# Second mixture's output products kind by kind over the row tiles of a chunk, in an attention and two-mixture kernel on one core

## The chip, the core and the metric

The kernel runs on one core of a Trainium2 chip. The metric is the device time of one execution in microseconds (us). The core has five engines: TensorE (PE, matrix products; its weight loads are listed as PEld), VectorE (DVE), ScalarE (ACT), GpSimd (POOL) and SyncE (SP, which here issues DMAs).

## The reference

Three stages follow each other. Attention over q, k, v of shape (4, 8, 576, 64) with a threshold: scores below the row maximum minus tau are dropped. The result, 2304 tokens of width 512, goes into a first mixture (512 to 1024 and back to 512 with a normalisation), and that into a second one, which is what the change touches:

```python
def _moe2_ref(x, w_in, w_out):
    h = x @ w_in                                        # 2304 x 512 by 512 x 2048
    g = np.maximum(h, 0.0) + np.log1p(np.exp(-np.abs(h)))
    return (g @ w_out).astype(np.float32)               # 2304 x 2048 by 2048 x 512
```

## The kernel before, in words

Matrix products use a high and a low part of every fp32 operand: x is split into `xh` and `xl`, the weights into `w2h`, `w2l` and `wo2h`, `wo2l`, g into `gh` and `gl`. A product of two numbers is made of three kinds, high by high, high by low and low by high, which are summed up in PSUM.

The second mixture goes over five blocks of tokens, four of 512 and one of 256, and in each over 16 chunks of 128 of the 2048 hidden columns. One chunk of one block has three steps.

- `m2_h` (line 573): twelve products into one PSUM bank give h for 128 hidden columns and all tokens of the block. ScalarE then takes Abs (L582) and Exp (L583), VectorE an add (L584) and a subtraction (L585), and ScalarE Ln (L586).
- `m2_g1`: VectorE takes a maximum and a sum (L591) and a subtraction (L592), ScalarE rounds to `gh` (L593), and VectorE forms `gl` (L594).
- `m2_y` (line 612): for each row tile j of 128 tokens, four in a large block and two in the last, three products of 128 x 512 into the bank `y{j}`. The bank collects all 16 chunks of a block. After the last chunk it is copied to `yo` (L616), by VectorE for even j and by ScalarE for odd j, and stored by a DMA that SP issues (L619).

The loop at the end of the function runs over all (block, chunk) pairs and looks two ahead: step i has `m2_h` of pair i, `m2_g1` of pair i - 1 and `m2_y` of pair i - 2. During block 0, `next(pw, 0)` also converts one chunk of w2_out per step (lines 80 to 88, on ScalarE, VectorE and POOL). In the later steps of a block, the x of the next one is loaded and split (L536, L541, L542).

The tile framework lays out the order of each engine when the program is built, and an engine's order in the trace deviates from the source in places. For instance, ScalarE runs Abs of the next chunk ahead of `gh` of this one.

Buffers that matter: four banks for h, one bank for each of `y0` to `y3`, three buffers each for `gh` and `gl`, and two for `yo`. So the first product into `y{j}` of a new block waits for the copy of the old `y{j}`, and the copy of tile 2 waits until the store of tile 0 has read its `yo`.

Of the kernel before, what the change touches and what calls it, by code (L numbers as in the profile page):

```python
# [21 lines left out]
P = 128  # L22
# [11 lines left out]
def tile_attention_solu_softplus(ctx: ExitStack, tc: tile.TileContext, q, k, v, tau, w_in, w_out, g_ln, w2_in, w2_out, out):  # L34
    nc = tc.nc
    PSUM = bass.MemoryType.PSUM
    pe, dve, act, pool, sp = nc.tensor, nc.vector, nc.scalar, nc.gpsimd, nc.sync
# [426 lines left out]
    NC2 = FF2 // P  # L464
# [95 lines left out]
    wo2h = [w2b.tile([P, DM], F32R, tag=f"wo2h{c}", name=f"wo2h{c}") for c in range(NC2)]  # L560
    wo2l = [w2b.tile([P, DM], F32R, tag=f"wo2l{c}", name=f"wo2l{c}") for c in range(NC2)]
    pw = prep_w2(w2a, lambda c: w2_out[c * P:(c + 1) * P, :].bitcast(U32), wo2h, wo2l, 2)
    gs = {}
    psy = {}
# [31 lines left out]
    def rows(bi, j):  # L596

        u, t = units[blocks[bi][0] + j // 2], j % 2
        if u == "T":
            return [(S * (2 * t + a) + 512, 64) for a in range(2)]  # L600
        return [(S * u[0] + 256 * u[1] + P * t, P)]

    def m2_y(bi, c):
        gl, gh = gs.pop((bi, c))[3:]
        n = blocks[bi][1]
        if c == 0:
            psy[bi] = [psY.tile([P, 512], F32, tag=f"y{j}", name=f"y{bi}_{j}") for j in range(n // P)]
        for j in range(n // P):
            y = psy[bi][j]
            i = 0  # L610
            for g_, w_ in ((gh, wo2h[c]), (gh, wo2l[c]), (gl, wo2h[c])):
                pe.matmul(y, g_[:, P * j:P * j + P], w_, start=(c == 0 and i == 0), stop=(c == NC2 - 1 and i == 2))  # L612
                i += 1
            if c == NC2 - 1:
                yo = m2.tile([P, DM], F32, tag="yo", name=f"yo{bi}_{j}", bufs=2)
                (act.copy if j % 2 else dve.tensor_copy)(out=yo, in_=y)  # L616
                r0 = 0
                for t0, m in rows(bi, j):
                    sp.dma_start(out=out[t0:t0 + m, :], in_=yo[r0:r0 + m, :])  # L619
                    r0 += m  # L620
# [3 lines left out]
    for i in range(len(seq) + LA):  # L624
        if i < len(seq):
            bi, c = seq[i]
            if bi == 0:
                next(pw, 0)
            if bi + 1 < len(blocks):
                j = (c - 2) // 4  # L630
                if c in (2, 6) and j < blocks[bi + 1][1] // 256:
                    m2_load(bi + 1, j)
                elif c in (4, 8) and j < blocks[bi + 1][1] // 256:
                    m2_split(bi + 1, j)
            m2_h(bi, c)
        if 0 <= i - 1 < len(seq):
            m2_g1(*seq[i - 1])
        if i >= LA:
            m2_y(*seq[i - LA])
# [51 lines left out]
```

## Time and profile before

| | |
|---|---|
| time, median of 3 runs | 1007.86 us (1007.46 to 1009.16) |
| the profiled execution's own time | 1010.33 us |
| its span, first to last instruction | 1008.5 us |
| mean granted TensorE clock in it | 0.971 |
| second mixture in it | about 600 to 1005 us; blocks change near 697, 790, 878 and 958 us |

The rows below come from the profiled execution. Times are counted from the start of its span. "Idle before" in brackets is how long the engine stood idle before an instruction, and behind the arrow is what ended that. A matmul's length contains its pipeline, so the rate of matmuls is read from their starts. A granted clock of 1.00 stands for 2.4 GHz, and 0.50 for 1.2 GHz.

### The profile page before, as it was taken

To read this page: it belongs to the slowest core of one execution; us is meant where nothing else is said; L and a number is where in the kernel's file an instruction comes from. 1 tells how busy PE (TensorE), PEld (TensorE's weight loads), DVE (VectorE), ACT (ScalarE), POOL (GpSimd) and SP (SyncE) were. 2 spreads that over 40 slices of the span, in tenths; PEclk is the share of its full clock that TensorE was granted. 3 is DMA by queue.
4 is the path that set the end of the run, shared out by engine and by line. 5 is a ranking of instruction groups with operands and counts; after the bars stand their busy time and mean duration, and the time that the engine had idled before them with its cause. 6 is when DMAs were issued, how large, how long until landed. Compare 5 with 4: busy or idle time off the path is not lost.

```text
span 1008.5 us, 14610 instructions
## 1 busy us (share of the span) xinstructions
PE 948.4 (94%) x5664; PEld 747.2 (74%) x5664; DVE 713.4 (71%) x1387; ACT 568.9 (56%) x1082; POOL 75.1 (7%) x47
## 2 busy tenths in 40 slices
PE   3898999999999999999997699898999999999997
PEld 2666567777677777876886588676888788888896
DVE  5898866766768577676589959976555755665565
ACT  4765666666657567566556546544444444444453
POOL 0000000000000000000033534311001000000000
PEclk8898899999999999999998799998999999999999
DMA  8412200112001220000054533302000100100010
GB/s 220 173 61 79 75 27 12 35 44 78 27 11 36 65 69 15 12 11 6 33 162 141 162 127 103 125 1 84 1 0 22 63 1 1 42 1 0 1 44 21
DMA packets 27125, 55.21 MB, mean 55 GB/s; under 512 B 3248, under 2 KB 12464, under 8 KB 27056
## 3 DMA queue, kind: packets, MB, share of 16 engines
q1 hardware_dynamic: 26896, 53.99, 17.1%
q8 instruction: 44, 0.72, 0.3%
q10 hardware_dynamic: 160, 0.30, 0.1%
q14 instruction: 25, 0.20, 0.1%
HBM read 44.83 MB, written 9.44 MB: 54 GB/s over the span
## 4 chain that ended last, share of the span: by engine, by line
PE 67%; DVE 18%; ACT 8%; issue 3%; DMA 2%; SPq 0%; DVEq 0%; ACTq 0%
PE y L612 12%; PE h L573 12%; PE s L177 10%; PE w L355 9%; PE w L403 8%; PE w L276 7%; PE w L210 5%; DVE u L82 2%; DVE w L584 2%; DVE t L585 2%; DVE w L591 2%; DMA raw<-in_w_in_dram 2%; DVE u L84 2%; DVE w L592 1%; DVE gl L594 1%
## 5 line engine op out<-in xcount | busy, mean ns | idle before, releaser
L177 PE MATMUL s<-k,q 64*128 64x288 f32 (+1 forms) x640 | 135.0, 445 | 16.8 <-ACT q L143 8.9
L187 DVE TENSOR_REDUCE nm<-s 128x1 f32<-128x576 f32 x144 | 104.5, 750 | 43.4 <-PE s L177 43.4
L573 PE MATMUL h<-x2h,w2h 128*128 128x512 f32 (+1 forms) x320 | 119.3, 375 | 8.6 <-ACT x2h L541 7.0
L188 ACT ACTIVATE E<-s,nm 128x576 f32<-128x576 f32 x128 | 92.5, 741 | 52.6 <-DVE nm L187 52.4
L612 PE MATMUL y<-wo2h,gh 128*128 128x512 f32 x288 | 114.6, 398 | 7.5 <-ACT gh L593 4.3
L573 PE MATMUL h<-x2l,w2h 128*128 128x512 f32 (+1 forms) x320 | 118.8, 371 | 0.8 <-POOL x2l L542 0.8
L573 PE MATMUL h<-x2h,w2l 128*128 128x512 f32 (+1 forms) x320 | 118.6, 371 | 0.0
L612 PE MATMUL y<-wo2h,gl 128*128 128x512 f32 x288 | 113.8, 397 | 4.6 <-DVE gl L594 4.6
L612 PE MATMUL y<-wo2l,gh 128*128 128x512 f32 x288 | 113.4, 394 | 0.0
L195 DVE SCALAR_TENSOR_TENSOR E<-E,etau 128x576 f32<-128x576 f32 x128 | 102.5, 813 | 13.0 <-ACT E L188 9.1
L177 PEld LDWEIGHTS s<-k,q 64*128 64x128 f32 (+1 forms) x640 | 71.1, 182 | 53.8 <-issue 13.1
L586 ACT ACTIVATE w<-w 128x512 f32<-128x512 f32 (+1 forms) x80 | 47.1, 589 | 96.5 <-DVE t L585 96.4
L593 ACT CAST gh<-w 128x512 fp32r<-128x512 f32 (+1 forms) x80 | 46.2, 577 | 84.6 <-DVE w L592 84.3
L212 ACT COPY eT<-w 128x512 f32<-128x512 f32 x128 | 72.0, 592 | 24.2 <-PE w L210 23.7
L403 PE MATMUL w<-lh,wo1h 128*128 128x256 f32 x288 | 83.6, 291 | 0.0
L276 PE MATMUL w<-eT,v 128*64 128x256 f32 (+2 forms) x784 | 83.1, 357 | 0.0
L591 DVE SCALAR_TENSOR_TENSOR w<-h,w 128x512 f32<-128x512 f32 (+1 forms) x80 | 50.9, 637 | 44.7 <-ACT w L586 44.7
L403 PE MATMUL w<-ll,wo1h 128*128 128x256 f32 x288 | 81.5, 283 | 0.0
L403 PE MATMUL w<-lh,wo1l 128*128 128x256 f32 x288 | 81.4, 283 | 0.0
L594 DVE TENSOR_TENSOR gl<-w,gh 128x512 fp32r<-128x512 f32 (+1 forms) x80 | 51.0, 638 | 42.2 <-ACT gh L593 41.5
L276 PEld LDWEIGHTS w<-eT,v 128*64 128x64 f32 x784 | 52.8, 140 | 32.9 <-issue 9.7
L573 PEld LDWEIGHTS h<-x2h,w2h 128*128 128x128 f32 x320 | 61.4, 192 | 20.3 <-ACT x2h L541 7.2
(100 smaller groups left out, 1870.1 us busy)
## 6 DMA issues: line engine op xcount, KB each, us to landing
raw<-in_w_in_dram SPq DMA_DIRECT2D x16, 512.0 KB, 3.5
raw<-in_w_out_dram SPq DMA_DIRECT2D x16, 512.0 KB, 3.5
v<-in_v_dram SPq DMA_DIRECT2D x16, 320.0 KB, 3.0
x2s<-x SPq DMA_DIRECT2D x36, 128.0 KB, 1.7
x2r<-x2s SPq DMA_DIRECT2D x9, 512.0 KB, 4.0
q<-in_q_dram SPq DMA_DIRECT2D x30, 144.0 KB, 3.0
raw<-in_w_in_dram SPq DMA_DIRECT2D x4, 1024.0 KB, 8.9
raw<-in_w_out_dram SPq DMA_DIRECT2D x4, 1024.0 KB, 5.0
```

Source lines behind the costliest of these rows:

```text
L177: pe.matmul(o, z["q"][r, c:c + m], z["k"][r, kc:kc + 288], start=True, stop=True)
L187: dve.tensor_reduce(out=nm, in_=sv, axis=AX.XY, op=ALU.max, negate=True)
L188: act.activation(out=E.rearrange("p (a b) -> p a b", a=2), in_=sv, func=AF.Exp, bias=nm, scale=1.0)
L195: dve.scalar_tensor_tensor(out=E, in0=E, scalar=etau, in1=E, op0=ALU.is_ge, op1=ALU.mult, accum_out=acc)
L212: act.copy(out=eT, in_=bk)
L276: pe.matmul(o[64 * h:64 * h + 64, :], w_, e, start=(i == 0), stop=(i == 4))
L355: pe.matmul(ps, x_[:, c, P * t:P * t + P], w_[:, c, 512 * n:512 * n + 512], start=(j == 0), stop=(j == 11))
L403: pe.matmul(o, w_[:, c, P * m:P * m + P], l_[:, c, :], start=(j == 0), stop=(j == 23))
L573: pe.matmul(ps, w_[:, kc, :], x_[:, kc, 0:n], start=(j == 0), stop=(j == 11))
L591: dve.scalar_tensor_tensor(out=w_, in0=ps, scalar=0.0, in1=w_, op0=ALU.max, op1=ALU.add)
L594: dve.tensor_tensor(out=gl, in0=w_, in1=f(gh), op=ALU.subtract)
L612: pe.matmul(y, g_[:, P * j:P * j + P], w_, start=(c == 0 and i == 0), stop=(c == NC2 - 1 and i == 2))
```

## The change

The three kinds of product of a chunk become the outer loop and the row tiles the inner one. The start flag stands at the first kind of chunk 0 and the stop flag at the last kind of chunk 15, as before. The copies and stores after the last chunk come behind all twelve products in the source.

```diff
         if c == 0:
             psy[bi] = [psY.tile([P, 512], F32, tag=f"y{j}", name=f"y{bi}_{j}") for j in range(n // P)]
+        for i, (g_, w_) in enumerate(((gh, wo2h[c]), (gh, wo2l[c]), (gl, wo2h[c]))):
+            for j in range(n // P):
+                pe.matmul(psy[bi][j], g_[:, P * j:P * j + P], w_, start=(c == 0 and i == 0), stop=(c == NC2 - 1 and i == 2))
         for j in range(n // P):
             y = psy[bi][j]
-            i = 0
-            for g_, w_ in ((gh, wo2h[c]), (gh, wo2l[c]), (gl, wo2h[c])):
-                pe.matmul(y, g_[:, P * j:P * j + P], w_, start=(c == 0 and i == 0), stop=(c == NC2 - 1 and i == 2))
-                i += 1
             if c == NC2 - 1:
```

## Rows read from the trace of the kernel before

**Rows 1.** The page, part 1: busy time, share of span, instructions.
```profile
PE 948.4 (94%) x5664; PEld 747.2 (74%) x5664; DVE 713.4 (71%) x1387; ACT 568.9 (56%) x1082; POOL 75.1 (7%) x47
```

**Rows 2.** The page, part 5: output products, first kind; busy, mean ns | idle before.
```profile
L612 PE MATMUL y<-wo2h,gh 128*128 128x512 f32 x288 | 114.6, 398 | 7.5 <-ACT gh L593 4.3
```

**Rows 3.** Waits, 600 to 1009 us: us in total, times, longest.
```profile
PE y L612 <- DVE gl L594: 4.6, 5, 1.9
PE y L612 <- ACT gh L593: 4.3, 6, 1.7
PE y L612 <- DVE yo L616: 3.2, 3, 1.7
```

**Rows 4.** Timeline of TensorE in block 0: start, length, instruction [idle before].
```profile
634.68 0.51 PE L612 MATMUL y<-wo2h,gl 128*128 128x512 f32 x1 [1.87 <-DVE gl L594]
...
637.01 0.63 PE L612 MATMUL y<-wo2l,gh 128*128 128x512 f32 x1
```

**Rows 5.** Stretches: length, busy PE, PEld, DVE, ACT, POOL, clock, DMA share, GB/s.
```profile
636.30:639.50 3.20, 3.20 (x9) 2.50 (x8) 3.10 (x7) 3.03 (x6) 0.11 (x1) 0.50 0.09 36
...
697.70:704.40 6.70, 5.63 (x13) 3.96 (x14) 4.55 (x9) 3.55 (x7) 0.00 (x0) 0.50 0.42 150
704.50:769.00 64.50, 64.50 (x286) 53.37 (x285) 38.02 (x60) 29.16 (x47) 0.00 (x0) 1.00 0.00 1
789.00:796.00 7.00, 5.31 (x24) 4.02 (x23) 4.85 (x9) 3.50 (x6) 0.00 (x0) 1.00 0.33 121
```

**Rows 6.** Waits, 603 to 697 us, the longest of ScalarE and of VectorE.
```profile
ACT w L586 <- DVE t L585: 20.3, 12, 3.0
...
DVE w L591 <- ACT w L586: 4.2, 6, 0.7
```

**Rows 7.** Timeline of TensorE where blocks change (0/1, 1/2, 2/3).
```profile
696.84 0.47 PE L612 MATMUL y<-wo2h,gh 128*128 128x512 f32 x1 [1.71 <-ACT gh L593]
...
700.58 0.80 PE L612 MATMUL y<-wo2h,gh 128*128 128x512 f32 x1 [1.07 <-DVE yo L616]
...
791.43 0.51 PE L612 MATMUL y<-wo2h,gh 128*128 128x512 f32 x1 [1.69 <-DVE yo L616]
...
879.24 0.50 PE L612 MATMUL y<-wo2h,gh 128*128 128x512 f32 x1 [0.43 <-DVE yo L616]
```

**Rows 8.** Timeline of VectorE at the change from block 0 to 1.
```profile
696.01 0.68 DVE L616 COPY yo<-y 128x512 f32<-128x512 f32 x1
...
697.85 0.69 DVE L585 SCALAR_TENSOR_TENSOR t<-w,t 128x512 f32<-128x512 f32 x1
...
699.84 0.68 DVE L616 COPY yo<-y 128x512 f32<-128x512 f32 x1
```

**Rows 9.** Timeline of ScalarE there, its second copy.
```profile
699.90 0.58 ACT L616 COPY yo<-y 128x512 f32<-128x512 f32 x1 [0.70 <-DMA out_dram<-yo]
```

**Rows 10.** The tile yo: its stores, from issue to landing.
```profile
DMA to landing us min/median/max: 2.0/2.2/4.4
```

**Rows 11.** Chain of waits in block 1: start, length, line; a y and an h chunk.
```profile
712.20 2.72 PE y L612 x12
714.92 2.72 PE h L573 x12
```

**Rows 12.** Timeline of ScalarE in block 4, its last wait for TensorE.
```profile
975.54 0.38 ACT L582 ACTIVATE t<-h 128x256 f32<-128x256 f32 x1 [0.24 <-PE h L573]
```

**Rows 13.** Timeline of the end, engine by engine.
```profile
1003.06 0.50 PE L612 MATMUL y<-wo2h,gh 128*128 128x512 f32 x1 [1.27 <-ACT gh L593]
...
1004.33 0.40 PE L612 MATMUL y<-wo2h,gl 128*128 128x512 f32 x1
1004.07 0.69 DVE L616 COPY yo<-y 128x512 f32<-128x512 f32 x1 [0.60 <-PE y L612]
1004.76 0.58 ACT L616 COPY yo<-y 128x512 f32<-128x512 f32 x1 [1.75 <-PE y L612]
1004.79 0.92 SPq L619 DMA_DIRECT2D out_dram<-yo  x2
```

## The prediction

> **What bounds the kernel now.** I read the page first: TensorE is busy for 94% of the span [rows 1], so a change must either take matmul time away or take away waits of TensorE. The change removes no product: the 864 products of line 612 (three groups of 288) stay, each with its weight load, and the lengths of one are about the same in the three groups, one of which stands in [rows 2]. So I looked at the waits of the second mixture, 600 to 1009 us. TensorE's own waits before line 612 have three releasers: `gl` (4.6 us in 5 waits), `gh` (4.3 us in 6) and the copies `yo` that free the banks of the block before (3.2 us in 3) [rows 3]. These 12.1 us are what an order of the output products can touch. The reader is to see where each of them lies.
>
> The `gl` waits lie in block 0, while w2_out is still being converted on VectorE. The longest is 1.87 us, between the second and the third product of a chunk, and a stretch at half clock follows it [rows 4]: granted clock 0.50 (1.2 GHz) from 636.3 to 639.5 us [rows 5]. The `yo` waits lie where one block of tokens follows another. There TensorE has done the six products of row tiles 0 and 1 of the new block and stands before tile 2, because VectorE has not yet copied the old tile 2 out: 1.07 us at 700.58, 1.69 at 791.43, 0.43 at 879.24 [rows 7]. The `gh` waits lie mainly ahead of 696.84 (1.71 us) [rows 7] and at the end.
>
> Next the question that decides the credit: who waits for TensorE? From 603 to 697 us the list of waits has eight rows of ScalarE and VectorE, and they name each other, POOL and one DMA, never TensorE (the two longest stand in [rows 6]). The chain Abs, Exp, add, subtract, Ln, max, subtract, `gh` runs there at its own pace, and `gh` of chunk 0 of block 1 comes at 696.84 whatever TensorE did before.
>
> **The change, part by part.**
>
> *Later need of `gl`.* A product takes 2.72/12 = 0.227 us [rows 11]. Before, `gl` is needed after two products of a chunk, after the change behind eight: 6 x 0.227 = 1.36 us more cover. Four of the five waits in block 0 (0.83, 0.25, 1.28, 0.37 in the timeline, against the 1.87) would vanish and the longest would shrink to 0.5. With the half-clock stretch (3.2 us at half rate, 1.6 us) that is up to 4.6 + 1.6 = 6.2 us of TensorE's time. I credit **0**: TensorE arrives earlier at the products at 689 and 696.84 us and waits there for `gh`, which does not depend on it [rows 6, 7]. The late one after the removed wait is `gh`. If that were wrong, the end is 6.2 us (first rival).
>
> *Change of bank with every product.* The new order writes another PSUM bank with each product, twelve changes a chunk instead of four. An h chunk (twelve products into one bank) and a y chunk (four banks) both take 2.72 us [rows 11], so a change costs under 0.01/4 us: **0**, at most 64 x 8 x 0.0025 = 1.3 us. The Trainium skill, page "TensorE: Matmul & The Clock Gate", section "A second HAM failure mode: psum-queue depth-cycling", reports a kernel at N=512 whose cycling through banks made short idle times and let the clock swing. That speaks against this change; here the trace disagrees as far as it goes, with a granted clock of 1.00 from 704.5 to 769 us [rows 5].
>
> *Same stationary twice.* `gh` of a tile is loaded for two products in a row before. Nothing is saved by that now: x288 loads stand beside x288 products. **0**.
>
> *When the banks of a block are complete.* This is the term that I charge. In the last chunk of a block, tile 0 is complete after product 3 now and after product 9 then (6 x 0.227 = 1.36 us later), tile 1 0.91 us and tile 2 0.45 us later, tile 3 as before. The four copies (tiles 0, 2 on VectorE, 1, 3 on ScalarE) have two buffers `yo`, so copy 2 also needs the store of copy 0 landed, 2.0 to 2.2 us after its issue [rows 10]; ScalarE's second copy has waited 0.70 us for just that [rows 9]. The store goes out on SP, where only `yo` and the x2 loads are queued. What stands behind a later copy in VectorE's queue is the next subtract, `gh` and `gl`.
>
> *When the next block needs its banks.* Its chunk 0 now needs tile 2 at its third product instead of its seventh, tile 3 at the fourth instead of the tenth. At 0/1, 1/2 and 2/3 TensorE already waits for tile 2. If the copies stay where they are, four products move from before that wait to behind it: 4 x 0.227 = 0.91 us each. Bounds: **0** if the framework, which orders the engines at build time, lays the products of tiles 0 and 1 ahead of tile 2; and 2.5 us if copy 0 falls behind the next long VectorE instruction. That is worked out at 0/1: copy 0 at 696.01 moves behind the operation at 697.85 that lasts 0.69, so to 698.5; 0.68 for itself, 2.2 for its store, 0.68 for copy 2 give 702.1 instead of 700.5 [rows 8, 10], 1.6 us, plus 0.91. Below 0 nothing is likely, for the copies can't start earlier. I take **1.4 us** for each of the three, nearest to the row where the copies stay, with half a microsecond for a copy that comes after one more VectorE operation: **+4.2 us**.
>
> *Boundary 3/4.* Block 4 has two tiles only; its chunk 0 does not need tiles 2 and 3, and ScalarE still waits 0.24 us for TensorE at 975.54 [rows 12], so a delay of the chain around 958 is caught up by then. **0**, at most 1.36 us.
>
> *The end.* The last chunk waits for `gh` until 1003.06 and then does six products [rows 13]: unchanged. Tile 0 is complete one product from the end instead of three; its copy ends at about 1005.2 instead of 1004.76, and its store goes out ahead of the other one on SP: **+0.25 us**, from 0 to 0.5.
>
> Sum: 4.2 + 0.25 = +4.45 us. On the profiled execution's own time of 1010.33 us (span 1008.5 and 1.8 around it) that is 1014.8. This execution lies 2.5 us above the median of the three runs, so I set the sum against the median: 1007.86 + 4.45 = **1012.3 us**.
>
> **The rivals.**
>
> 1. *Faster: the removed `gl` waits pay.* Place: block 0, 632 to 662 us. Price: 4.6 us, with the half clock 6.2; the end would be 1007.9 - 6.2 + up to 4.5, about 1002 to 1005. It decides where `gh` at 689 and 696.84 turns out to follow TensorE. Against it: no wait for TensorE in 603 to 697 [rows 6]. For it: the build-time order of VectorE may change along and shorten the chain. Chance 0.10.
> 2. *No difference.* The build-time order already deviates from the source where a bank or operand is not ready (in block 0 some `gh` products stand ahead of `gl`), and could keep six products before tile 2. Then the loss is 0 to 0.5 a boundary: about 1008.5 us. Chance 0.28.
> 3. *Slower still, by the clock.* TensorE would stand for 2.6 us and more at a boundary. A wait of 1.71 us at 696.84 was followed by 0.50 from 697.7 to 704.4, while 1.69 us at 791.43 left it at 1.00 [rows 5, 7]. Another such stretch at 1/2 and 2/3 costs 1.7 to 3.4 us each: 1014 to 1019. Chance 0.14.
> 4. *Bank cycling brings the clock down*, the page's rule above, as a mechanism of this kernel: y products at half rate would add up to 864 x 0.227, far over 1100 us. The row at 1.00 speaks against it. Chance 0.02.
>
> **How the numbers follow.** The forecast (1009.9 to 1014) has 0.46, slower by the three boundaries. The range 1006.0 to 1018.0 holds it, the second rival and most of the third; left out are most of the first and the fourth. About 0.2%, 2 us, is what a measurement of this kernel can tell from no change. Faster by more: rival 1, 0.10. Within: rival 2, 0.28. Slower: 0.46 + 0.14 + 0.02 = 0.62.
>
> **What would show it.** Right: `gl` waits of TensorE nearly gone, `gh` waits ahead of 697 us larger by about as much; `yo` waits up from 3.2 to some 7 us, at the first products of tile 2 or 3; last copy 0.2 us later against the last product. Wrong: block 1 starts its output products before 696.8 (first rival), or `yo` waits unchanged (second). y chunks longer than 2.72 us in mid-block would refute the free change of bank.

## The result and the profile after

The changed kernel takes 1016.35 us (median of 5 runs, 1014.16 to 1019.29) against 1007.86 us before: a ratio of 1.0085, interval [1.0068, 1.0102], so 8.6 us slower by the ratio and 8.5 by the medians. The forecast was 1012.3 us, slower. The direction came out, and the size is about twice the forecast: 1016.35 us lies above the 1009.9 to 1014 of the forecast itself, and within the stated range of 1006 to 1018. The profiled execution took 1019.15 us (span 1017.4 us, mean granted clock 0.968 against 0.971); it lies 2.8 us above its median and that of before 2.5 above its own, so the two profiles may be compared row by row.

In the changed kernel the output products are line 610, the copies line 615 and the stores line 618. TensorE does the same number of products (x5664 on the page, as in [rows 1]). In the second mixture, what grew above all is its waits, which answer to [rows 3]: the list of waits of TensorE, 600 to 1018 us (us in total, times, longest).

```profile
PE y L610 <- DVE yo L615: 9.7, 5, 3.7
PE y L610 <- ACT gh L593: 8.0, 9, 1.3
PE y L610 <- DVE gl L594: 1.6, 3, 0.8
...
PE y L610 <- ACT yo L615: 0.5, 1, 0.5
```

Two things are to be seen. The `gl` waits fell by 3.0 us and the `gh` waits rose by 3.7: what the new order saves in block 0 is given back, as the prediction had it. And the waits for the copies `yo` rose from 3.2 to 10.2 us, by 7.0 us, which is most of the 8.9 us by which the spans differ.

Where the loss lies can be read from one row per block, its first output product. The timeline of TensorE before (block 1's first product, at 696.84, stands in [rows 7], and the start of the last six products, 1003.06, in [rows 13]):

```profile
603.20 0.50 PE L612 MATMUL y<-wo2h,gh 128*128 128x512 f32 x1 [0.24 <-ACT gh L593]
...
788.20 0.39 PE L612 MATMUL y<-wo2h,gh 128*128 128x512 f32 x1
...
877.29 0.39 PE L612 MATMUL y<-wo2h,gh 128*128 128x512 f32 x1
...
961.24 0.40 PE L612 MATMUL y<-wo2h,gh 128*128 128x512 f32 x1
```

And after, with the products that waited where blocks change. They answer to [rows 7]; "x2" in a row means two products merged into one row.

```profile
602.52 0.50 PE L610 MATMUL y<-wo2h,gh 128*128 128x512 f32 x1 [0.28 <-ACT gh L593]
...
699.28 0.70 PE L610 MATMUL y<-wo2h,gh 128*128 128x512 f32 x2 [3.70 <-DVE yo L615]
...
702.50 0.80 PE L610 MATMUL y<-wo2h,gh 128*128 128x512 f32 x1 [2.07 <-DVE yo L615]
...
792.28 0.70 PE L610 MATMUL y<-wo2h,gh 128*128 128x512 f32 x2 [1.06 <-DVE yo L615]
...
795.51 0.51 PE L610 MATMUL y<-wo2h,gh 128*128 128x512 f32 x1 [2.06 <-DVE yo L615]
...
883.38 0.62 PE L610 MATMUL y<-wo2h,gh 128*128 128x512 f32 x2
...
885.28 0.50 PE L610 MATMUL y<-wo2h,gh 128*128 128x512 f32 x1 [0.81 <-DVE yo L615]
...
886.96 0.50 PE L610 MATMUL y<-wo2h,gh 128*128 128x512 f32 x1 [0.48 <-ACT yo L615]
...
968.52 0.40 PE L610 MATMUL y<-wo2h,gh 128*128 128x512 f32 x1
...
1011.42 0.73 PE L610 MATMUL y<-wo2h,gh 128*128 128x512 f32 x2 [1.27 <-ACT gh L593]
```

From first product to first product:

| stretch | before, us | after, us | longer by |
|---|---|---|---|
| block 0, with the wait at the start of block 1 | 93.64 | 96.76 | 3.12 |
| block 1, with the wait at the start of block 2 | 91.36 | 93.00 | 1.64 |
| block 2 | 89.09 | 91.10 | 2.01 |
| block 3 | 83.95 | 85.14 | 1.19 |
| block 4 up to its last six products | 41.82 | 42.90 | 1.08 |

So the loss comes at every block change, and the first product of blocks 1 and 2 now waits too: not for `gh`, but for the copy of tile 0. The timeline of VectorE after, at the change from block 0 to 1, answers to [rows 8]:

```profile
697.51 0.69 DVE L594 TENSOR_TENSOR gl<-w,gh 128x512 fp32r<-128x512 f32 x1 [0.68 <-ACT gh L593]
698.12 0.42 DVE L584 TENSOR_SCALAR w<-t 128x512 f32<-128x512 f32 x1
698.45 0.68 DVE L615 COPY yo<-y 128x512 f32<-128x512 f32 x1
...
701.16 0.69 DVE L592 TENSOR_TENSOR w<-w,t 128x512 f32<-128x512 f32 x1
701.77 0.68 DVE L615 COPY yo<-y 128x512 f32<-128x512 f32 x1
```

TensorE had written the last product of the old block before the h products that end at about 695.6 us, so the bank was long complete. Yet VectorE waits 0.68 us for `gh`, does `gl` and the add, and only then copies tile 0. Before, the copy stood ahead of these two. Then it filled that idle time: it ran at 696.01 [rows 8], and `gl` followed without a wait. Tile 2's copy, ahead of the subtraction of L592 before, stands behind it now. ScalarE's copy of tile 3, which was ahead of Abs and `gh`, moved behind `gh`. So it is at 1/2 too, and nothing else changed its order on these engines there. At 2/3, copy 0 falls behind the add and the subtraction of L585, and copy 3, which was behind `gh` already, behind Abs and Exp; copy 2 keeps its place. The products were not made slower in mid-block, and the granted clock is 1.00 there; it is 0.50 in two stretches behind the waits (stretches after, columns as in [rows 5]):

```profile
700.60:707.40 6.80, 4.89 (x12) 3.88 (x13) 5.01 (x8) 3.10 (x6) 0.00 (x0) 0.50 0.34 124
707.50:780.00 72.50, 72.50 (x322) 60.01 (x321) 41.97 (x63) 31.86 (x51) 2.40 (x1) 1.00 0.00 1
...
796.20:799.60 3.40, 3.40 (x10) 2.62 (x9) 2.31 (x5) 0.95 (x2) 0.00 (x0) 0.50 0.45 159
```

At the change to block 4, ScalarE's last copy waits for a store and holds up ScalarE's chain; at the end the copies come later against the last products. Timelines of ScalarE and SP after, which answer to [rows 12] and [rows 13]:

```profile
972.11 0.58 ACT L615 COPY yo<-y 128x512 f32<-128x512 f32 x1 [1.33 <-DMA out_dram<-yo]
...
1013.60 0.82 SPq L618 DMA_DIRECT2D out_dram<-yo  x2
```

From the last six products to the last stores' issue it is 13.60 - 11.42 = 2.18 us, against 4.79 - 3.06 = 1.73 before: +0.45 us.

### The profile page after: what moved, and what is told of

It is laid out like the page before. It is cut to its first block, busy times and chain, and to the rows that moved or that the text cites. A ratio compares the mean times of both kernels' runs of the same rounds, so it can differ in the third digit from the quotient of the medians.

```text
span 1017.4 us, 14616 instructions
## 1 busy us (share of the span) xinstructions
PE 952.6 (94%) x5664; PEld 748.7 (74%) x5664; DVE 714.0 (70%) x1387; ACT 568.9 (56%) x1082; POOL 73.2 (7%) x47
## 4 chain that ended last, share of the span: by engine, by line
PE 64%; DVE 19%; ACT 10%; issue 4%; DMA 2%; SPq 0%; POOL 0%; DVEq 0%; ACTq 0%
PE h L573 11%; PE y L610 11%; PE s L177 10%; PE w L355 9%; PE w L403 8%; PE w L276 7%; PE w L210 5%; DVE t L585 2%; DVE u L82 2%; DVE w L584 2%; DVE w L591 2%; DVE w L592 2%; ACT w L586 2%; DMA raw<-in_w_in_dram 1%; DVE u L84 1%
## 5 line engine op out<-in xcount | busy, mean ns | idle before, releaser
L177 PE MATMUL s<-k,q 64*128 64x288 f32 (+1 forms) x640 | 138.1, 452 | 15.3 <-ACT q L143 8.8
L610 PE MATMUL y<-wo2h,gh 128*128 128x512 f32 x288 | 82.6, 401 | 18.1 <-DVE yo L615 9.7
L610 PE MATMUL y<-wo2h,gl 128*128 128x512 f32 x288 | 81.3, 398 | 1.6 <-DVE gl L594 1.6
L584 DVE TENSOR_SCALAR w<-t 128x512 f32<-128x512 f32 (+1 forms) x80 | 42.5, 532 | 54.0 <-ACT t L583 44.9
L610 PE MATMUL y<-wo2l,gh 128*128 128x512 f32 x288 | 80.2, 392 | 0.0
L610 PEld LDWEIGHTS y<-wo2h,gh 128*128 128x128 f32 x288 | 52.4, 189 | 34.2 <-ACT gh L593 12.2
```

What stands on the lines that cost most here:

```text
L177: pe.matmul(o, z["q"][r, c:c + m], z["k"][r, kc:kc + 288], start=True, stop=True)
L610: pe.matmul(psy[bi][j], g_[:, P * j:P * j + P], w_, start=(c == 0 and i == 0), stop=(c == NC2 - 1 and i == 2))
```

## The experiments

The times below are medians; every ratio is to the kernel before as run beside it (medians of 1008.05 to 1009.16 us), so 0.001 is 1 us; it isn't exactly the ratio of the two medians. "Waits for yo" are TensorE's in the one profiled execution, with the copies of both engines added.

| run | what it is | us | ratio, interval | waits for yo, us |
|---|---|---|---|---|
| | before | 1007.86 | 1 | 3.2 |
| | the whole change | 1016.35 | 1.0085 [1.0068, 1.0102] | 10.2 |
| e1 | by kind in chunks 1 to 14 only | 1008.18 | 0.9999 [0.9989, 1.001] | 3.2 |
| e2 | by kind in chunk 15 only | 1014.3 | 1.0057 [1.0034, 1.008] | 7.7 |
| e3 | by kind in chunk 0 only | 1014.1 | 1.0054 [1.0037, 1.007] | 6.1 |
| e4 | whole change, four `yo` | 1009.04 | 1.0008 [0.9996, 1.002] | 5.1 |
| e5 | before, four `yo` | 1003.27 | 0.9949 [0.9929, 0.9969] | 0 |
| e6 | e1 with four `yo` | 1003.59 | 0.9951 [0.9934, 0.9968] | 0 |
| e7 | e2, copies held in their old places | 1010.67 | 1.0028 [1.0014, 1.0041] | 3.2 |
| e8 | e3 with four `yo` | 1005.12 | 0.9975 [0.9957, 0.9993] | 0.7 |
| e9 | whole change, copies held | 1009.81 | 1.0013 [1.0002, 1.0025] | 3.6 |
| e10 | whole change, copies held, four `yo` | 1005.85 | 0.997 [0.9959, 0.9981] | 0.8 |
| e11 | before, copies in the changed kernel's places | 1012.28 | 1.0033 [1.0022, 1.0043] | 8.4 |

### The change cut into its parts

The same edit serves e1, e2, e3, e6, e7 and e8; only the condition differs. Shown is e1's; it is `c == NC2 - 1` in e2 and `c == 0` in e3. `prod(i, j)` is the product of kind i and row tile j.

```diff
...
+        by_kind = 0 < c < NC2 - 1
+        if by_kind:
+            for i in range(3):
+                for j in range(n // P):
+                    prod(i, j)
         for j in range(n // P):
             y = psy[bi][j]
-            i = 0
-            for g_, w_ in ((gh, wo2h[c]), (gh, wo2l[c]), (gl, wo2h[c])):
-                pe.matmul(y, g_[:, P * j:P * j + P], w_, start=(c == 0 and i == 0), stop=(c == NC2 - 1 and i == 2))
-                i += 1
+            if not by_kind:
+                for i in range(3):
+                    prod(i, j)
```

**Chunks 1 to 14 (e1).**

> Kind by kind in chunks 1 to 14 of every block, tile by tile in chunk 0 and in chunk 15. Theory A (all of the loss of 8.5 us arises where blocks change, and the gl waits of block 0 are given back to gh waits): 1007.9 us as before, within 1 us; gl waits of TensorE fall from 4.6 to under 2 us, gh waits rise by about as much, yo waits stay at 3.2 us. Rival B (the order itself costs in mid-block, by the change of bank or of operand): at least 3 us slower than before, y chunks longer than 2.72 us. Rival C (the removed gl waits pay): 1002 to 1003.5 us.

The ratio is 0.9999 [0.9989, 1.001]: no loss and no gain, as theory A has it. Waits of TensorE, 600 to 1018 us:

```profile
PE y L612 <- ACT gh L593: 7.9, 10, 1.7
PE y L612 <- DVE yo L625: 3.2, 3, 1.7
PE y L612 <- DVE gl L594: 1.6, 3, 0.8
```

`gl` gave up 3.0 us and `gh` took 3.6, almost as in the whole change, and the waits for `yo` are those of before. From its first output product to that of block 1, block 0 takes 694.54 - 600.95 = 93.59 us, against 93.64 before. An output chunk with a new bank for every product lasts what it did, by the chain of waits of this run in block 1 (compare [rows 11]):

```profile
704.49 2.72 PE y L612 x12
```

So the order within a block costs nothing and brings nothing, and the loss belongs to the first and the last chunk.

**Chunk 15 (e2).**

> Kind by kind in chunk 15 of every block alone; the copies lie on VectorE and ScalarE where they lie after the whole change. Theory A with the late copies as the main part: 6 to 8 us slower than before (1014 to 1016), yo waits of TensorE 8 to 11 us. Rival D (the early need of tiles 2 and 3 in chunk 0 is the main part): at most 2 us slower than before.

1.0057, or 5.7 us: a little under the 6 to 8 of theory A, with waits a little under its 8 to 11, and far over rival D's 2. (The profiled execution, 1011.86 us, was the shortest of the four.) Its rows at the first two block changes show the new wait of the first product:

```profile
695.95 0.77 PE L612 MATMUL y<-wo2h,gh 128*128 128x512 f32 x1 [3.65 <-DVE yo L625]
...
787.46 0.47 PE L612 MATMUL y<-wo2h,gh 128*128 128x512 f32 x1 [1.06 <-DVE yo L625]
```

3.65 and 1.06 us are the whole change's 3.70 and 1.06. In this kernel, too, the copies stand behind `gl` and the add on VectorE, and behind `gh` on ScalarE.

**Chunk 0 (e3).**

> Kind by kind in chunk 0 of every block alone; the copies stay where they were before the change. Theory A with the late copies as the main part: 0 to 1.4 us slower than before (at most two products of 0.227 us less ahead of each of three waits for tile 2). Rival D (the early need of tiles 2 and 3 is the main part): 5 us slower or more. My forecast's own step, four products behind the wait at each boundary, would give 2.7 us.

1.0054, or 5.4 us. Theory A had 0 to 1.4 us and the prediction's own step 2.7; rival D's 5 or more came true here. As e2 costs as much, neither of the two parts is the main one. Here the copies stay where they were, but TensorE's order is strictly by kind: only two products stand ahead of tile 2 in place of six. The waits at tile 2 (before, [rows 7]: 1.07, 1.69, 0.43) are longer by about four products, 0.91 us, at 1/2 by less:

```profile
698.77 1.22 PE L612 MATMUL y<-wo2h,gh 128*128 128x512 f32 x2 [1.97 <-DVE yo L625]
...
790.50 0.73 PE L612 MATMUL y<-wo2h,gh 128*128 128x512 f32 x2 [2.27 <-DVE yo L625]
...
880.78 1.03 PE L612 MATMUL y<-wo2h,gh 128*128 128x512 f32 x2 [1.34 <-DVE yo L625]
```

That makes 0.90 + 0.58 + 0.91 = 2.4 us, and 0.5 for a wait for ScalarE's copy of tile 1. The stretch behind the second wait ran at half clock, which it did not before, at a cost of some 3.4/2 = 1.7 us in this execution:

```profile
791.40:794.80 3.40, 3.40 (x10) 2.66 (x9) 2.33 (x4) 1.46 (x3) 0.00 (x0) 0.50 0.42 151
```

The parts don't add up to the whole (5.7 + 5.4 against 8.6). The three intervals together are wide enough for that, and there is a likely reason, too. In the whole change the framework lays four products (both `gh` kinds of tiles 0 and 1) ahead of tile 2, not two, so the early need costs it less than it costs e3.

### The buffers

**The whole change with four `yo` (e4).**

```diff
-                yo = m2.tile([P, DM], F32, tag="yo", name=f"yo{bi}_{j}", bufs=2)
+                yo = m2.tile([P, DM], F32, tag="yo", name=f"yo{bi}_{j}", bufs=4)
```

> The whole change with four buffers yo instead of two: copy 2 needs no landed store and lies two VectorE operations earlier, copy 0 stays. Theory A: the second wait at each boundary (2.07, 2.06 and 0.81 us) shrinks to under 0.5, so 4 us of the 8.5 come back, 1011 to 1013 us. Rival E (copy 0 alone is what counts, or the store is no limit): under 1 us comes back, 1015.5 to 1017.

1.0008: nearly all of the 8.6 us comes back, well over the 4 us expected. Taken alone that reads as if two buffers were the cause. The rows say something else. Copy 0 is as late as in the changed kernel, and the first product waits as long; only the second wait is gone:

```profile
698.04 2.33 PE L610 MATMUL y<-wo2h,gh 128*128 128x512 f32 x4 [3.69 <-DVE yo L615]
```

**The kernel before with four `yo` (e5)** decides it, with the same edit.

> The kernel before, with four buffers for yo instead of two. Theory S (the second copy of each engine waits at a block change for the store of the first one, through the two buffers, and so the bank of tile 2 comes free late): TensorE's waits for yo at tile 2, 1.07 + 1.69 + 0.43 = 3.2 us in the kernel before, shrink to under 1 us, and the time falls by 2 to 3 us, to 1005 to 1006 us. If the copies of tiles 2 and 3 were late for another reason (their place in the queues of VectorE and ScalarE), the waits stay at about 3 us and the time within 1 us of 1008.

0.9949, 5.1 us faster than before and more than was expected. So the buffers pay in either order of the products, and with four of them the change still costs 1.0008 - 0.9949, or 5.9 us. The list of waits for this kernel has no row for `yo` on TensorE at all. On VectorE copy 2 stands at 697.42, right behind the add (before: 699.84 [rows 8]), and the stretch that ran at half clock before [rows 5] runs at full clock:

```profile
697.08 0.42 DVE L584 TENSOR_SCALAR w<-t 128x512 f32<-128x512 f32 x1
697.42 0.68 DVE L616 COPY yo<-y 128x512 f32<-128x512 f32 x1
```

```profile
694.00:704.00 10.00, 8.29 (x35) 6.19 (x34) 7.36 (x13) 5.84 (x11) 0.00 (x0) 1.00 0.44 156
```

3.2 us of waits and up to half of the 6.7 us at half clock make 3.2 to 6.6 us, which holds the 5.1; how the 5.1 splits between the two is not shown.

**Chunks 1 to 14 by kind, four `yo` (e6).** e1 and e5 together.

> Four buffers for yo, and kind by kind in chunks 1 to 14 only. Chunks 1 to 14 by kind alone gave 0.9999 of the time before, so theory S expects what the kernel before with four buffers gives, 1005 to 1006 us, within 0.7 us of it. If the earlier products in block 0 can pay once the block change no longer stops TensorE, it is 1 us or more faster than that.

0.9951 [0.9934, 0.9968], the same as e5 alone, as expected. The order within a block stays worth nothing with the block change cleared: its `gh` waits are still 7.9 us.

**Chunk 0 by kind, four `yo` (e8).** e3 and e5 together.

> Chunk 0 alone kind by kind, four buffers for yo. Chunk 0 by kind with two buffers was 5.5 us slower than before: TensorE stood before tile 2 with four of its products still undone that had covered the wait. Theory S: with four buffers the copy of tile 2 no longer waits for a store, so the early need of tile 2 costs under 1 us a block change and the time is within 2 us of the kernel before, 1006 to 1010 us. If the early need costs by itself, whatever the buffers, it stays 4 us or more slower, at 1012 us or more.

0.9975: 2.6 us above e5, where e3 is 5.4 us above before. That would be half the cost of the early need once copy 2 doesn't wait for a store; but the intervals of e8 and e5 overlap, so it may also be less or nothing. The waits at 0/1 and 1/2 are down to 0.49 and 0.17 us; the first of them:

```profile
698.78 1.88 PE L612 MATMUL y<-wo2h,gh 128*128 128x512 f32 x3 [0.49 <-ACT yo L625]
```

These are less than 2.6 us. In this execution 698.30 to 705.10 us ran at a granted clock of 0.50, which e5 did not have; that would be up to 3.4 us. But this execution, 1009.03 us, lies 3.9 us above the median, and whether the stretch comes in every one is not shown.

### The place of the copies

**Chunk 15 by kind, copies held (e7).** Edges that only fix the order make later instructions of VectorE and ScalarE stand behind the copies, at the first three block changes.

```diff
+    def hold(ins, copy):
+        tc.add_manual_dep(ins, copy.name, mybir.DependencyInfo(mybir.DependencyClass.NoSync, mybir.DependencyReason.DATA), reason="place of the copy")
...
+                if j == 0 and bi < 3:
+                    hold(add1[bi + 1], copy)
+                    if bi < 2:
+                        hold(gl0[bi + 1], copy)
```

`add1` is the add (L584) of chunk 1 of the new block and `gl0` the `gl` of its chunk 0: copy 0 comes ahead of both. In the same way copy 2 is held ahead of L592 of chunk 1 and copy 3 ahead of Abs of chunk 2.

> Chunk 15 alone kind by kind, with two buffers as before, but the copies stand at the block changes 0/1, 1/2 and 2/3 in the places among the instructions of VectorE and ScalarE that they have in the kernel before. Chunk 15 by kind without this was 5.8 us slower than before. If the cost is the place that a copy falls back to in its queue, this kernel loses only what is left: about 0.5 us at the end and 0.9 us at 3/4, so 1009 to 1010 us. If the cost is that the banks of tiles 0 and 1 are complete 1.36 and 0.91 us later, whatever the place, it stays 4 us or more slower than before, at 1012 us or more; VectorE and ScalarE then wait for TensorE ahead of their first copies by 0.5 us and more.

1.0028 [1.0014, 1.0041]: half of e2's loss is gone (2.9 us, by the two intervals good to some 2.7). The waits for `yo` are back at 3.2 us in sum, and no copy of these three block changes waits for TensorE: the banks are complete early enough, though by the order of the products tile 0's is complete six products (1.36 us) later than before.

```profile
700.46 0.50 PE L624 MATMUL y<-wo2h,gl 128*128 128x512 f32 x1 [0.85 <-DVE gl L604]
...
703.05 0.50 PE L624 MATMUL y<-wo2h,gh 128*128 128x512 f32 x1 [1.39 <-DVE yo L637]
...
789.91 0.50 PE L624 MATMUL y<-wo2h,gl 128*128 128x512 f32 x1 [0.44 <-DVE gl L604]
```

That speaks against the theory that lateness of the banks itself costs. What is left is more than the 1 to 2 us expected by a little, and the two `gl` rows show a reason. With these edges `gl` of chunk 0 fell behind the add, which waits for ScalarE, so TensorE waits for `gl` at its third product, 0.85 us at 0/1 and 0.44 at 1/2. Before, it has no such waits there. So this run keeps somewhat more than what the place of the copies leaves over.

**The kernel before, copies put into the changed kernel's places (e11),** is the converse: TensorE's order is that of before, product by product.

```diff
...
+        if c == 1 and bi in (1, 2):
+            hold(copies[bi - 1, 2], ins)
+        ins = act.copy(out=gh, in_=w_).ins
+        if c == 1 and bi in (1, 2, 3):
+            hold(copies[bi - 1, 3], ins)
...
+                if j == 0 and bi < 3:
+                    hold(copy, add1[bi + 1])
```

`hold` puts its first argument behind its second, so now the copies are the ones that stand behind. `ins` is L592 of chunk 1 in the first case, `gh` in the second. (At 2/3 it is the subtraction of L585, not the add, that copy 0 is put behind.)

> The kernel before, its products untouched and its order on TensorE the same, two buffers; only the copies at 0/1, 1/2 and 2/3 are put into the places in VectorE's and ScalarE's queues that they have in the changed kernel. If the place alone is what chunk 15 by kind costs (5.8 us, of which 0.5 at the end and 0.9 at 3/4 lie elsewhere), this kernel is 4 to 5 us slower than before, with waits of TensorE for yo of about 7 us. If the place costs only together with tiles that are complete later, it is within 1.5 us of the kernel before.

1.0033 [1.0022, 1.0043]: the place alone costs 3.3 us, a little under the 4 to 5 expected, and brings the same waits (3.42 and 1.06 us of first products, 3.70 and 1.06 in the changed kernel):

```profile
700.35 0.47 PE L624 MATMUL y<-wo2h,gh 128*128 128x512 f32 x1 [3.42 <-DVE yo L628]
...
792.83 0.47 PE L624 MATMUL y<-wo2h,gh 128*128 128x512 f32 x1 [1.06 <-DVE yo L628]
```

**The whole change, copies held, two and four buffers (e9, e10).** As e7 with the change in every chunk; at 3/4 copy 0 is held too, and one more edge keeps `gl` of chunk 0 ahead of the add, as it is before. e10 also has four buffers, with copy 2 ahead of the subtraction of chunk 1, where e5 has it.

> The whole change, two buffers, but at the four block changes the copies stand in VectorE's and ScalarE's queues where they stand in the kernel before. The whole change was 8.5 us slower than before. If two parts add up, the place that the copies fall back to (5.8 us with chunk 15 alone by kind, 2.8 us once the copies were held) and the early need of tile 2 (5.4 us with chunk 0 alone by kind), this kernel keeps the second part and the 0.5 us of the end: 4 to 6 us slower than before, 1012 to 1014 us. If the copies are late because tiles 0 and 1 are complete later, it stays at 8 to 9 us slower, about 1016 us.

1.0013 [1.0002, 1.0025]: 7.2 of the 8.6 us come back, more than expected. The rows show why the early need of tile 2 is not left over:

```profile
696.75 0.47 PE L626 MATMUL y<-wo2h,gh 128*128 128x512 f32 x1 [2.00 <-ACT gh L603]
...
697.72 0.50 PE L626 MATMUL y<-wo2h,gh 128*128 128x512 f32 x1 [0.49 <-ACT yo L639]
698.05 0.62 PE L626 MATMUL y<-wo2l,gh 128*128 128x512 f32 x2
698.52 0.63 PE L626 MATMUL y<-wo2h,gl 128*128 128x512 f32 x2
700.49 0.72 PE L626 MATMUL y<-wo2h,gh 128*128 128x512 f32 x2 [1.34 <-DVE yo L639]
```

With the copies held, the framework lays all six products of tiles 0 and 1 ahead of tile 2 again, `gl` products among them. So this run does not part the place from the early need: the edges brought both back.

> The whole change with both remedies: four buffers for yo, and the copies in the places that they have in the kernel before with four buffers (which took 1003.3 us). If place and buffers are all that the change costs besides the end, it takes 1003.5 to 1005 us, 0.5 to 1.5 us more than that kernel, with waits of TensorE for yo under 1 us in sum. If the order of the products costs something of its own at a block change, it stays near the whole change with four buffers and the copies left where they fall, 1009 us.

0.997 [0.9959, 0.9981], 2.1 us above e5 and 3.8 us below e4; expected were 0.5 to 1.5 above e5, and 2.1 is within the noise of the two. The second figure is the price of the place once more, with four buffers. With four, the framework is again strictly by kind in chunk 0, as in e8 (2.6 us above e5), and its waits at 0/1 are as small: 0.49 and 0.16 us.

The best version is neither kernel of the case but the one before with four buffers, 1003.27 us; e6, 1003.59, can't be told from it.

## Why the prediction was right, and where it was too small

| term | predicted, us | measured |
|---|---|---|
| later need of `gl`, in block 0 | 0 | 0 (e1: 0.9999) |
| change of bank; same stationary | 0, at most 1.3 | 0 (e1) |
| copies fall back in their queues, 0/1 to 2/3 | 0.5 x 3 = 1.5 | 3.3 (e11, interval 2.2 to 4.3) |
| tile 2 needed earlier | 0.91 x 3 = 2.7 | some 2.9 in the whole (8.6 less e2's 5.7); 5.4 alone (e3) |
| boundary 3/4 | 0, at most 1.36 | 1.08 in the rows |
| the end | 0.25, at most 0.5 | 0.45 in the rows |

**The number.** 1016.35 us is outside the forecast's own 1009.9 to 1014. The range held it only by the room left for the third rival (1014 to 1019, by the clock), and the clock is not shown to be what brought it there: see below. That the range held is in part luck; what was right is the direction, and where the loss arises.

**Later need of `gl`: right.** It was the step on which the sign hung. The `gl` waits fell from 4.6 to 1.6 us, the `gh` waits took their place, and the time stood still with the new order alone (e1) and with the block changes cleared (e6). The first rival falls. One loss in block 0 does not come from the order of the products. Of the 3.12 us of the table's first line, 1.7 go with the place of the copies: in e2 and e4, which share it, that stretch is 95.33 us. The other 1.4 are missing there and present in e11 (96.77 us), whose order on TensorE is that of before. They arise in the chain of VectorE, and the first of them shows here, 2.3 us behind the first product, before:

```profile
605.50 0.68 DVE L585 SCALAR_TENSOR_TENSOR t<-w,t 128x512 f32<-128x512 f32 x1
605.32 3.55 POOL L88 TENSOR_TENSOR wo2l<-u,wo2h 128x512 fp32r<-128x512 f32 x1 [3.97 <-ACT wo2h L87]
```

and after:

```profile
604.81 1.79 DVE L585 SCALAR_TENSOR_TENSOR t<-w,t 128x512 f32<-128x512 f32 x1
604.63 1.42 POOL L88 TENSOR_TENSOR wo2l<-u,wo2h 128x512 fp32r<-128x512 f32 x1 [3.96 <-ACT wo2h L87]
```

Both engines have the same order in both kernels up to there. Where the two operations overlap, one of them is drawn out: POOL's before (so in e2 and e4), VectorE's after (so in e11). The delay of 1 to 1.5 us that this leaves in block 0 stands in the profiles of the changed kernel, e7, e9, e10 and e11, and in none of the others. What decides it, and whether it comes in every execution of these five, is not shown. If it did, it would be in e11's 3.3 us and in the whole 8.6 as well.

**Change of bank: right.** Chunks of 2.72 us and a granted clock of 1.00 in mid-block, 707.5 to 780 us of the changed kernel, refute the fourth rival. The rule of the Trainium skill, told there of a bf16 kernel, that cycling through banks makes short idle times and lets the clock swing ("TensorE: Matmul & The Clock Gate", "A second HAM failure mode: psum-queue depth-cycling") does not show itself in this kernel: e1's interval, 0.9989 to 1.001, leaves room for 1 us at most.

**The banks and their copies: right in mechanism, mis-sized.** The step that failed is "I take 1.4 us for each of the three, nearest to the row where the copies stay, with half a microsecond for a copy that comes after one more VectorE operation". Its own upper end, 2.5 us with copy 0 behind a long VectorE instruction, was the nearer: 3.12, 1.64 and 2.01 us were lost up to the changes and through them, of which the first holds the 1.4 that are not of the order, and the third up to 1.7 of a new half-clock stretch. At 0/1 and 1/2 copy 0 fell behind two instructions, `gl` and the add. Worse, `gl` waits for `gh` there (0.68 us), so the copy waits behind a stalled instruction. And the prediction moved only copy 0 behind another instruction: copies 2 and 3 went back too. It looked for the waits at tiles 2 and 3 alone, while 3.70 + 1.06 of the 10.2 us stand at the first product of a block, for copy 0. It took as cause that the banks are complete later in time. e7 shows that this lateness did no harm by itself, for no held copy waits for TensorE at these changes; the cost came with the order that was laid out at build time. Whether that order follows from the later products, or from the copies' new place in the source behind all twelve of them, no run separates.

**The early need: right as a wait, but not by the working that was given.** The prediction had four products moving behind the wait. In the whole change it is two (four stand ahead of tile 2 in place of six), but with the copies later. With two ahead (e3) the waits grew by 0.90, 0.58 and 0.91 us, about as worked out, and the clock added to it.

**The clock (third rival) came in part at most.** One new stretch of 3.4 us at half clock, from 796.2 us, is worth up to 1.7 us. The half-clock stretch of block 0 [rows 5] is missing in the changed kernel, so in that one execution the two cancel: what is left are the waits, 7.7 us more in sum over `yo`, `gh` and `gl`. For the other executions nothing shows how much of the 8.6 us is the clock's.

**Boundary 3/4: the zero was wrong,** inside its bound. The delay was to be caught up by ScalarE's waits for TensorE. But ScalarE's copy of tile 3 waited 1.33 us for a store in the middle of its chain, and after as before TensorE stands for `gh` before the last six products. With four buffers the stretch from the first product of block 4 to the last six is 1002.37 - 960.40 = 41.97 us in e4, against 41.82 before; so it was this store, as far as one execution of each shows.

```profile
960.40 0.40 PE L610 MATMUL y<-wo2h,gh 128*128 128x512 f32 x1
...
1002.37 0.50 PE L610 MATMUL y<-wo2h,gh 128*128 128x512 f32 x1 [1.26 <-ACT gh L593]
```

**No difference (second rival)** fell as a whole, since only four products stand ahead of tile 2; but its mechanism exists, for e9 has the six.

Together: the place of the copies 3.3, the early need 2.9, the change to block 4 about 1.1 and the end 0.45 make 7.7 of 8.6 us. As the 2.9 are themselves a difference, what this sum tests is e2: the other three make 4.8 of its 5.7. The intervals of e2 and of the whole change are 2.3 and 1.7 us to either side, so the 2.9 are known to some 2.9 only, and the delay in block 0 named above may be in the 3.3. That both parts cost something rests on e11 and e3.

## What to carry to other kernels

When an accumulation is reordered, ask what it does to the place of the evictions in the queues of the engines that do them: a framework that orders at build time may put a copy behind an instruction that itself stalls, and then the loss includes the stall, not only the few products by which the bank is later. A reordering that covers a wait pays only if the producer waits for the consumer somewhere; where the producer's chain runs at its own pace, the wait comes back under another name. And look at the number of output buffers first: four in place of two were worth 5.1 us in the old order and 7.7 in the new one, which in the new order alone looks like the cause of the whole loss.

## What was not expected of the hardware

How much TensorE stands does not by itself tell whether the granted clock falls. Before, waits of 1.71 and 1.07 us around 697 to 701 us came with 0.50 for 6.7 us [rows 5, 7]. In e9 there were 2.00, 0.49 and 1.34 us in the same place, and the whole stretch shows 1.00:

```profile
690.00:707.00 17.00, 13.17 (x56) 10.01 (x56) 12.35 (x18) 8.93 (x16) 2.39 (x1) 1.00 0.27 94
```

The kernel before has 0.80 over the same 17 us in its profile. Its executions beside e11 had mean granted clocks from 0.966 to 0.978, the lowest of them in one of the longest (1010.33 us). So part of the difference between single executions may be this stretch at half clock; that, and what brings it on in one and not in another, stays open.
